# Small matmuls of a fused attention and feed-forward kernel, gathered into fewer visits of the matmul engine

## The chip, the core and the metric

The kernel runs on one core of one Trainium2 chip. The metric is device time in microseconds (us) of one execution, and the median of three runs of the kernel before is 529.8 us (529.61 to 529.82). The core has a matmul engine (TensorE, PE in the profile, with its weight loads shown apart as PEld), three elementwise engines (VectorE or DVE, ScalarE or ACT, GpSimd or POOL), a queue engine (SP) that issues all transfers here, and 16 DMA engines. TensorE writes only into PSUM, which holds eight banks of 128 x 512 words. Each engine executes its own instructions in program order and waits for others by semaphores.

## The reference

The computation is an attention against 32 pooled memories per head, followed by a bilinear feed-forward network on the attention's output:

```python
a = softmax(phi, axis=sequence)                # per batch and head: 576 x 32
k_m, v_m = a.T @ k, a.T @ v                    # 32 memories of 64
scores = q @ k_m.T / sqrt(64)                  # 576 x 32
attn = softmax(scores)                         # over the 32 memories
x = (attn @ v_m), heads side by side           # 4608 x 512 in all
out = ((x @ w1) * (x @ w2)) @ w3 @ w_out       # w1, w2: 512 x 1024
```

There are 8 batches, 8 heads, 576 rows per batch, and everything is float32 (the kernel keeps float32 accuracy by splitting numbers into a high and a low part and multiplying three times).

## The kernel before

The kernel never forms x. It uses that x @ w1 equals attn @ (v_m @ w1), so for each batch it computes a matrix **M**, the memories' values times w1 and w2, and multiplies the probabilities by M. It also computes the product W = w3 @ w_out once, at the start. M is made in four **quarters** of its columns (M0 to M3 in the tables of steps), each from a quarter of w1 and w2.

For each batch there are two long stages of full-size matmuls. The **ab stage** (`ab_stage`, line 675 for the matmuls) multiplies probabilities by M, with a scheme of seven products in place of eight, over eight column blocks f = 0 to 7. It uses for the first block the first quarter M0, and for the last two the quarter M3. Its first products are called q1 and q5, and q5 needs a bank named `o`. The **out stage** (`out_stage`, line 779) multiplies its result g by W in blocks of 128 rows. One block is 24 matmuls of 128x128 by 128x512 into one bank `o` of two, which ScalarE then copies to `osb` (line 789) and SP sends out. One `O` in the tables is a quarter of a block, six matmuls. Odd batches have five blocks, even ones four.

Between these `O`s the out stage of batch b places the attention steps of batch b+1, in the order of the table `REST`. Each name in it goes one step on with a generator:

- `blocks` turns the memories, so that lines 297 and 298 can write km (keys) and vm (values). `mem` (lines 267 and 276), which makes the memories, stands at the end of the ab stage.
- `sc0` and `sc1` (line 310) are the scores of the two halves of the rows, each 8 small matmuls of 64x32 by 64x288 (16 instructions in the trace, since a float32 matmul is issued as two). sc0 goes into the two banks of the pair `x`, sc1 into two banks `a`.
- `se`, `sn` and `pr` are the softmax on VectorE, with one exponential each on ScalarE; `pr1` ends it with a transpose into `at` (line 349).
- `ps` makes sums of the probabilities on GpSimd (line 364), their high parts on ScalarE and low parts on GpSimd (lines 366 and 367). q5 needs the last of these.
- `M0` to `M3` (`memory_weights`) have four steps: 8 small matmuls of 64x32 by 64x512 (line 386) into one bank `a` and one bank `b`; three copies on ScalarE (lines 432 and 434); six differences on VectorE (lines 437 and 439); and a cast on ScalarE (line 441) with two differences on GpSimd (line 444).
- `W0` to `W3` (`stage`, line 415) fetch a quarter of w1 and w2 back from memory, 1 MB each, into tiles that other steps use too: W0 and W3 into `kv0`, W1 into `kv2`, W2 into `q`. So W2 follows the scores, which read q, and W3 follows M0.
- `phi2`, `rows2`, `q2` and `kv2` are the loads for batch b+2.

The order on all engines is written by hand. It is the order in which the Python code runs, so the table fixes it for PE, VectorE, ScalarE, GpSimd and SP alike. The table `START` does the same for everything before the first out stage, the ab stage of batch 0 (line 646) included; its names are units A and B of that stage, steps with the batch behind a dot (`mem.1`), and others.

The PSUM banks are two `a`, two `b` (`ps_ab`), two `o` (`ps_o`) and the pair `x` (`ps_x`).

Of the kernel before, what the change touches and what calls it, by code (L numbers as in the profile page):

```python
# [36 lines left out]
K11 N1 pr0.0 W17 K12 N1 A0 K13 K10 B0 K12 A0 sc1.0 K13 A0 A4 S0 S1 L24 C23 A0 phi1 B4 A4 L25 rows1 S2 A0 A1 A4 sc1.0 A4 B1 A1  # L37
A4 N2 A1 se1.0 A1 A5 N2 A1 se1.0 B5 A5 N2 C24 se1.0 A5 A9 K10 A5 B9 sn1.0 A9 C24 sn1.0 A8 sn1.0 B8 C25 A9 pr1.0 O0 A9
A5 A8 A9 pr1.0 A8 O0 C25 pr1.0 top.1 row.1 A8 kv1 A11 kv1 B11 kv1 A8 A11 exp.1 C25 q1 A6 phi2 A11 exp.1 C25 B6 A11 A6
A3 A11 A6 B3 A3 norm.1 A6 C24 A10 A6 A3 B10 A10 C24 S3 A3 A7 A3 N3 A7 A10 A10 B7 N3 A10 O0 A7 N3 A7 A2 A7 A15 less.1 A2  # L40
B15 A15 A14 less.1 A15 A15 B14 A15 B2 A13 less.1 A2 A14 A2 A14 A13 A2 A14 less.1 B13 A14 A12 A13 A13 less.1 B12 A13
A12 mem.1 A12 A12 A12 mem.1
""".split()
MEETS = {0: "<M3 top", 1: "top exp", 2: "exp row", 3: "norm", 5: "less less", 6: "less less", 7: "less"}
REST = """
W0 W1 O blocks blocks O sc0 sc1 sc0 W2 se0 se0 sc1 se0 O se1 se1 se1 O M0 W3 phi2 rows2 sn0 sn0 sn0 pr0 M0 M0 O M1 M0 M1
sn1 sn1 sn1 pr1 O O ps M1 M2 q2 M2 O ps M1 O M2 O M3 kv2 M3 M2 O M3 M3
""".split()


# [1 line left out]
def memory_attention__then__bilinear_ffn_kernel(  # L52
# [24 lines left out]
    NT = 2  # L77
# [13 lines left out]
    ps_ab = ctx.enter_context(tc.tile_pool(name="ps_ab", bufs=2, space=bass.MemoryType.PSUM))  # L91
# [23 lines left out]
    def psum(pool, name):  # L115
        return pool.tile([P, 512], F32, name=name, tag=name)

    def psum_pair():
        return ps_x.tile([P, 2, 512], F32, name="x")

    def pair():
        x = psum_pair()
        return [x[:, i] for i in range(2)]

    def banks_ab():

        return [psum(ps_ab, x) for x in "ab"]
# [254 lines left out]
    def weights_times(b, q, w, ps):  # L382
        for g in range(NG):
            for t in range(NT):
                d = slice((1 - t) * D, (2 - t) * D)
                nc.tensor.matmul(
                    ps[t][g * M : (g + 1) * M], lhsT=vm[b % 2][d, g], rhs=w[d, :, g], start=True, stop=True
                )
# [27 lines left out]
        staged[q] = x.rearrange("p (w g f) -> p w g f", w=2, g=NG)  # L416

    def memory_weights(b, q):
        ps = banks_ab()
        weights_times(b, q, staged[q], ps)  # L420
        (b12, b11), (b21, b22) = [[x[:, k * FQ : (k + 1) * FQ] for k in range(2)] for x in ps]
        yield
        if "x" not in staged:
            staged["x"] = const.tile([P, 2, 4, FQ], F32, name="x", tag=f"w12_{NQ - 1}")
        if q == 2:
            x = const.tile([P, CW], F32, name="u", bufs=2).rearrange("p (k f) -> p k f", k=4)
        else:
            x = staged["x"][:, int(q == 1)]
        t1, t2, t3, t4 = [x[:, k] for k in range(4)]
        mh, ml = ready["M", b][q] = [new.tile([P, 7, FQ], F32R, name=f"{z}{q}") for z in ("mh", "ml")]  # L430
        firsts = ((0, 1, b11), (1, 3, ps[1].rearrange("p (k f) -> p k f", k=2)))
        nc.scalar.copy(out=t4, in_=b12)
        for i, j, y in firsts:
            nc.scalar.copy(out=mh[:, i:j], in_=y)
        yield
        for y, p, r in ((t1, t4, b11), (t3, b22, t4), (t2, b22, t1), (t4, b21, t2)):
            nc.vector.tensor_tensor(out=y, in0=p, in1=r, op=ALU.subtract)  # L437
        for i, j, y in firsts:
            nc.vector.tensor_tensor(out=ml[:, i:j], in0=y, in1=mh[:, i:j].bitcast(F32), op=ALU.subtract)
        yield  # L440
        nc.scalar.copy(out=mh[:, 3:], in_=x)  # L441
        for k in range(0, 4, 2):
            y = slice(3 + k, 5 + k)
            nc.gpsimd.tensor_tensor(out=ml[:, y], in0=x[:, k : k + 2], in1=mh[:, y].bitcast(F32), op=ALU.subtract)  # L444
# [138 lines left out]
    under_way = {}  # L583
# [161 lines left out]
    def ab_stage(b, go, before, part):  # L745
# [4 lines left out]
        for p in range(NF + 2):  # L750
            for x in order:
                if x == "+":
                    for what in MEETS.get(p, "").split():
                        if what[0] == "<":
# [48 lines left out]
    new = ctx.enter_context(tc.tile_pool(name="new", bufs=1, side="right", reuse_waits="tile"))  # L803

    def goer(b):
        begun = {}

        def go(what):
            if b + 1 == B:
                return  # L810
            if what not in begun:
                if what[0] == "M":
                    begun[what] = memory_weights(b + 1, int(what[1]))
                else:
                    begun[what] = steps[b + 1][what]()
            next(begun[what], None)

        return go
# [12 lines left out]
    def out_stage(b, go):  # L831
        ready["M", b + 1] = {}
        part, left = out_parts(b), 4 * ((S + b % 2 * REST_ROWS) // P)
        if b == 0:
            left -= 3
        next(part)
        for what in REST + left * ["O"]:
            if what == "O":
                if left > (b + 1 < B):
                    left -= 1  # L840
                    next(part)
            elif what[:-1] in LOADS:
                whole(load(what, b))
            elif what[0] == "W":
                if b + 1 < B:
                    stage(int(what[1]))
            else:
                go(what)
        return part
# [77 lines left out]
```

## Time and profile before

| What | Value |
|---|---|
| median of 3 runs | 529.8 us (529.61 to 529.82) |
| the profiled execution | 529.76 us, its span 528.0 us |
| granted TensorE clock | 1.00 (2.4 GHz) |
| PE busy | 516.9 us (98%) |
| PEld busy | 407.2 us (77%) |
| DVE busy | 360.9 us (68%) |
| ACT busy | 295.4 us (56%) |
| POOL busy | 205.4 us (39%) |
| DMA moved | 103.29 MB, 196 GB/s |

The page also shows the chain of work that ended last, the groups of instructions with their durations, and, beyond it, the trace gives a timeline, waits, and busy times of any stretch. Matmuls are pipelined, so the time one of them takes on TensorE is read from start to start in the timeline, and not from its duration. A busy PE can be a PE that drains.

### The profile page before, as it was taken

What the parts mean: (1) busy time and instruction counts of PE and PEld (TensorE: products, weight loads), DVE (VectorE), ACT (ScalarE), POOL (GpSimd) and SP (SyncE); (2) the same over time, 40 slices, a digit from 0 to 9 for tenths busy, and PEclk for the clock granted to TensorE, in tenths of its full rate; (3) what the DMA queues carried; (4) which work ended last, traced back from release to release, by engine and by line L of the source; (5) the groups of instructions that cost most, each with busy time, mean ns of one, the idle gap of its engine ahead of it and who ended that gap; (6) DMA issues with size and microseconds to landing.
All of it is one profiled execution on the core that took longest, in us unless ns stands there. A gap on an engine that the chain in (4) does not pass through costs nothing.

```text
span 528.0 us, 10212 instructions
## 1 busy us (share of the span) xinstructions
PE 516.9 (98%) x3879; PEld 407.2 (77%) x3879; DVE 360.9 (68%) x741; ACT 295.4 (56%) x574; POOL 205.4 (39%) x161
## 2 busy tenths in 40 slices
PE   8999999998999999999999999999999999999997
PEld 5447688856986699659975899669966898679986
DVE  4889999597759647695769366885768285955500
ACT  6998976437643656256625465366536364365411
POOL 0000000018641934257534924286427644195500
DMA  8999776896237810685057600783069403510011
GB/s 334 420 415 422 315 256 235 329 367 210 106 122 279 336 47 8 242 308 210 11 224 292 242 32 10 308 338 114 2 253 338 183 17 131 210 41 22 1 40 60
DMA packets 21825, 103.29 MB, mean 196 GB/s; under 512 B 2577, under 2 KB 3729, under 8 KB 12817
## 3 DMA queue, kind: packets, MB, share of 16 engines
q1 hardware_dynamic: 21776, 102.65, 50.9%
q8 instruction: 30, 0.49, 0.4%
q14 instruction: 19, 0.15, 0.1%
HBM read 89.00 MB, written 13.64 MB: 194 GB/s over the span
## 4 chain that ended last, share of the span: by engine, by line
PE 65%; DVE 22%; DMA 5%; issue 4%; ACT 2%; POOL 1%; SPq 0%; ACTq 0%; DVEq 0%
PE o L779 22%; PE b L675 13%; PE o L675 8%; PE a L675 8%; DMA kv<-in_weights 4%; DVE s_sb L341 3%; PE x L267 3%; DVE s_sb L320 2%; DVE small L327 2%; DVE s_sb L329 2%; PE a L561 2%; DVE x L437 2%; PE b L561 2%; DVE small L336 2%; DVE small L338 1%
## 5 line engine op out<-in xcount | busy, mean ns | idle before, releaser
L743 POOL TENSOR_TENSOR gl<-u,gh 128x576 fp32r<-128x576 f32 x56 | 79.7, 1428 | 105.9 <-ACT gh L740 100.8
L779 PE MATMUL o<-W,gh 128*128 128x512 f32 (+1 forms) x296 | 100.3, 393 | 0.0
L444 POOL TENSOR_TENSOR ml<-x,mh 128x512 fp32r<-128x512 f32 x42 | 53.5, 1295 | 120.2 <-ACT mh L441 120.2
L779 PEld LDWEIGHTS o<-W,gh 128*128 128x128 f32 x296 | 55.1, 188 | 25.1 <-issue 14.7
L675 PE MATMUL b<-ahl,mh 128*128 128x288 f32 x336 | 73.5, 301 | 0.2 <-DVE gr L725 0.2
L779 PE MATMUL o<-Wh,gh 128*128 128x512 f32 (+1 forms) x148 | 59.2, 400 | 0.0
L779 PE MATMUL o<-Wl,gh 128*128 128x512 f32 (+1 forms) x148 | 57.1, 386 | 0.0
L779 PE MATMUL o<-W,gl 128*128 128x512 f32 (+1 forms) x148 | 56.9, 384 | 0.0
L779 PE MATMUL o<-Wh,gl 128*128 128x512 f32 (+1 forms) x148 | 56.9, 384 | 0.0
L675 PEld LDWEIGHTS b<-ahl,mh 128*128 128x128 f32 x336 | 53.9, 188 | 2.9 <-issue 1.2
L717 DVE TENSOR_TENSOR o<-b,a_sb 128x288 f32<-128x288 f32 x56 | 25.8, 461 | 40.7 <-PE b L675 40.7
L675 PE MATMUL b<-ahl,ml 128*128 128x288 f32 x168 | 49.6, 295 | 0.0
L675 PE MATMUL o<-ahl,mh 128*128 128x288 f32 x224 | 48.3, 296 | 0.9 <-POOL ahl L367 0.9
L675 PE MATMUL a<-ahl,mh 128*128 128x288 f32 x224 | 47.8, 295 | 0.0
L694 ACT COPY b<-a 128x288 f32<-128x288 f32 x56 | 21.5, 383 | 38.4 <-DVE u L733 21.1
L789 ACT COPY osb<-o 128x512 f32<-128x512 f32 (+1 forms) x37 | 21.3, 574 | 38.6 <-PE o L779 30.6
L733 DVE TENSOR_TENSOR u<-b,gr 128x288 f32<-128x288 f32 x56 | 25.6, 458 | 24.6 <-PE b L675 24.4
L725 DVE TENSOR_TENSOR gr<-b,a_sb 128x288 f32<-128x288 f32 x56 | 25.4, 454 | 22.8 <-PE b L675 22.1
L779 PEld LDWEIGHTS o<-Wh,gh 128*128 128x128 f32 x148 | 27.8, 188 | 16.7 <-issue 11.4
L740 ACT CAST gh<-u 128x576 fp32r<-128x576 f32 x56 | 37.4, 679 | 1.6 <-DVE u L733 1.6
L675 PEld LDWEIGHTS o<-ahl,mh 128*128 128x128 f32 x224 | 36.0, 188 | 1.1 <-POOL ahl L367 1.1
L675 PEld LDWEIGHTS a<-ahl,mh 128*128 128x128 f32 x224 | 36.4, 188 | 0.6
(169 smaller groups left out, 1171.3 us busy)
## 6 DMA issues: line engine op xcount, KB each, us to landing
kv<-kept SPq DMA_DIRECT2D x21, 1024.0 KB
kv<-in_kv SPq DMA_DIRECT2D x16, 1024.0 KB, 8.2
raw<-in_weights SPq DMA_DIRECT2D x10, 1024.0 KB, 19.5
q<-in_qT SPq DMA_DIRECT2D x8, 1152.0 KB
out<-osb SPq DMA_DIRECT2D x31, 256.0 KB, 2.0
q<-kept SPq DMA_DIRECT2D x7, 1024.0 KB, 5.5
raw<-in_weights SPq DMA_DIRECT2D x12, 512.0 KB, 4.2
ph<-in_phiT SPq DMA_DIRECT2D x9, 576.0 KB, 10.0
```

Of the source, the lines that this page charges most:

```text
L267: nc.tensor.matmul(ps[t][h * M : (h + 1) * M, : 2 * D], lhsT=v["a"][:, i, t, h * M : (h + 1) * M], rhs=kvt[i][:, (4 * t + h) * 2 * D : (4 ...
L444: nc.gpsimd.tensor_tensor(out=ml[:, y], in0=x[:, k : k + 2], in1=mh[:, y].bitcast(F32), op=ALU.subtract)
L561: nc.tensor.matmul(pw[r][i], lhsT=x[:, i * P : (i + 1) * P], rhs=y, start=k == 0 and j == 0, stop=k == NF - 1 and j == len(pairs) - 1,)
L675: nc.tensor.matmul(ps, lhsT=x[:, j], rhs=y[:, i], start=start and k == 0, stop=stop and k == 2, skip_group_check=True,)
L694: nc.scalar.copy(out=self.u, in_=self.a)
L717: nc.vector.tensor_tensor(out=self.c, in0=self.u, in1=self.s5, op=ALU.add)
L725: nc.vector.tensor_tensor(out=self.c22, in0=self.u, in1=self.s5, op=ALU.add)
L733: nc.vector.tensor_tensor(out=self.gr[:, 1], in0=self.u, in1=self.c22, op=ALU.mult)
L740: nc.scalar.copy(out=self.cut(gh), in_=self.gr)
L743: nc.gpsimd.tensor_tensor(out=self.cut(gl), in0=self.gr, in1=self.cut(gh).bitcast(F32), op=ALU.subtract)
L779: nc.tensor.matmul(ps, lhsT=x[f][:, at : at + P], rhs=y[f][:, cols], start=f == 0 and k == 0, stop=f == NF - 1 and k == 2,)
L789: nc.scalar.copy(out=osb[:, cols], in_=ps)
```

## The change

Three things move; no instruction is removed or added in the stages named above, apart from where merged rows are counted.

First, `REST` takes M0's matmuls directly behind sc1's, and puts M1's, M3's and M2's directly behind one another, after six further `O`s (36 matmuls). Second, the banks: M0 now takes both banks `b`, M1 both banks `a`, M2 both banks `b`, and M3 the pair `x`, in place of one `a` and one `b` each. W3 is fetched directly behind W2. M0's differences now stand inside `sn0`, and its cast behind `ps`' first cast. Third, for batch 1 alone, `less`, `mem` and `blocks` move into the ab stage of batch 0 in `START`, between its units, and a table `REST0` of its own orders the first out stage: there the scores stand at its head, M0 stands alone 12 matmuls later, and M1, M3 and M2 follow together 30 matmuls behind it.

```diff
-A3 A11 A6 B3 A3 norm.1 A6 C24 A10 A6 A3 B10 A10 C24 S3 A3 A7 A3 N3 A7 A10 A10 B7 N3 A10 O0 A7 N3 A7 A2 A7 A15 less.1 A2
-B15 A15 A14 less.1 A15 A15 B14 A15 B2 A13 less.1 A2 A14 A2 A14 A13 A2 A14 less.1 B13 A14 A12 A13 A13 less.1 B12 A13
-A12 mem.1 A12 A12 A12 mem.1
+A3 A11 A6 B3 A3 norm.1 A6 C24 A10 A6 A3 B10 A10 C24 S3 A3 A7 A3 N3 A7 A10 A10 B7 N3 A10 O0 A7 less.1 N3 A7 A2 A7 A15 less.1 less.1 A2
+B15 A15 A14 less.1 A15 A15 B14 A15 less.1 B2 A13 A2 A14 mem.1 A2 A14 A13 mem.1 A2 A14 B13 A14 blocks.1 A12 A13 A13 blocks.1
+B12 A13 A12 A12 A12 A12
...
+REST0 = """
+W0 W1 sc0 sc1 sc0 W2 se0 se0 O sc1 se0 O se1 se1 se1 M0 W3 sn0 sn0 sn0 pr0 O M0 sn1 sn1 sn1 pr1 ps M0 phi2 rows2 O M0 O O O M1 M3 M2 q2 kv2 M1
+ps M1 M1 O M2 O M2 M2 O M3 O M3
+""".split()
 REST = """
-W0 W1 O blocks blocks O sc0 sc1 sc0 W2 se0 se0 sc1 se0 O se1 se1 se1 O M0 W3 phi2 rows2 sn0 sn0 sn0 pr0 M0 M0 O M1 M0 M1
-sn1 sn1 sn1 pr1 O O ps M1 M2 q2 M2 O ps M1 O M2 O M3 kv2 M3 M2 O M3 M3
+W0 W1 O blocks blocks O sc0 sc1 M0 sc0 W2 W3 se0 se0 se0 sc1 O M0 se1 se1 se1 sn0 sn0 M0 sn0 pr0 O sn1 sn1 sn1 pr1 ps M0 phi2 rows2 O O O O M1 M3 M2 q2 kv2 M1
+ps M1 M1 O M2 O M2 M2 O M3 O M3
 """.split()
...
     def memory_weights(b, q):
-        ps = banks_ab()
+        ps = pair() if q == 3 else [psum(ps_ab, "bab"[q]) for _ in range(NT)]
...
     def goer(b):
-        begun = {}
+        begun = {x[:-2]: step for x, step in under_way.items() if b == 0 and x.endswith(".1")}
...
-        for what in REST + left * ["O"]:
+        for what in (REST if b else REST0) + left * ["O"]:
```

The first place is TensorE in the out stage of batch 2, which prepares batch 3. Names are out<-weights or moving tile; `kv_2454` and the like are the staged quarters, and `x8` counts matmuls of the program with the same names. Before, behind the second scores:

```order
L310 MATMUL a<-q,km_83 32x288 x8
L779 MATMUL o<-W_587,gh_618 128x512
...
L386 MATMUL a<-kv_2454,vm_85 32x512
L386 MATMUL b<-kv_2454,vm_85 32x512
...
L779 MATMUL o<-Wh_90,gh_614 128x512
...
L386 MATMUL a<-kv_2456,vm_85 32x512
...
L386 MATMUL a<-q,vm_85 32x512
...
L386 MATMUL a<-kv_2535,vm_85 32x512
...
```

Now, behind the same scores (all line numbers are four higher):

```order
L314 MATMUL a<-q,km_83 32x288 x8
L390 MATMUL b<-kv_2452,vm_85 32x512 x8
L783 MATMUL o<-W_587,gh_618 128x512
...
L783 MATMUL o<-W_590,gh_621 128x512
L390 MATMUL a<-kv_2454,vm_85 32x512 x8
L390 MATMUL x<-kv_2510,vm_85 32x512 x8
L390 MATMUL b<-q,vm_85 32x512 x8
L783 MATMUL o<-Wh_90,gh_614 128x512
```

Before, the scores and the four quarters were five visits, with 12, 6, 12 and 18 matmuls of the out stage between them. Now they are two visits with 36 between them, and 42 follow the second one up to q1 (66 in the longer out stages of odd batches).

The second place is ScalarE in the same out stage, from the first cast of the probabilities on. Before:

```order
L366 CAST ahl<-at 128x864
L432 COPY u<-a 128x256
L434 CAST mh_2628<-a 128x256
...
L789 COPY osb<-o 128x512
L366 CAST ahl<-sums 128x1152
L441 CAST mh_2578<-x 128x1024
L432 COPY x<-a 128x256
...
L441 CAST mh_2628<-u 128x1024
L441 CAST mh_2682<-x 128x1024
L789 COPY osb<-o 128x512
L694 COPY b<-a 128x288
```

Now:

```order
L370 CAST ahl<-at 128x864
L445 CAST mh_2523<-x 128x1024
L793 COPY osb<-o 128x512
L436 COPY x<-a 128x256
...
L370 CAST ahl<-sums 128x1152
L445 CAST mh_2638<-x 128x1024
L436 COPY u<-b 128x256
...
L445 CAST mh_2662<-u 128x1024
L436 COPY x<-x 128x256
...
L793 COPY osb<-o 128x512
L698 COPY b<-a 128x288
```

The copies of three quarters (the second `x<-a`, `u<-b` and `x<-x`) and two of the out stage's own copies (`osb<-o`) now all stand behind the cast that waits for the softmax's end, where before two quarters had been copied ahead of it.

## Rows read from the trace of the kernel before

**Rows 1.** The page's first part: busy us, share of span, instructions of each engine.

```profile
PE 516.9 (98%) x3879; PEld 407.2 (77%) x3879; DVE 360.9 (68%) x741; ACT 295.4 (56%) x574; POOL 205.4 (39%) x161
```

**Rows 2.** The page's chain of work that ended last, by line.

```profile
PE o L779 22%; PE b L675 13%; PE o L675 8%; PE a L675 8%; DMA kv<-in_weights 4%; DVE s_sb L341 3%; PE x L267 3%; DVE s_sb L320 2%; DVE small L327 2%; DVE s_sb L329 2%; PE a L561 2%; DVE x L437 2%; PE b L561 2%; DVE small L336 2%; DVE small L338 1%
```

**Rows 3.** Waits of PE: waited for, us in total, times, longest us.

```profile
PE a L386 <- ACT mh L434: 3.5, 7, 0.5
PE o L675 <- POOL ahl L367: 0.9, 1, 0.9
```

**Rows 4.** Timeline of PE, one out stage: start us, duration us, instruction, [idle before].

```profile
217.41 0.72 PE L310 MATMUL x<-q,km 64*32 64x288 f32 x16
217.92 0.69 PE L310 MATMUL a<-q,km 64*32 64x288 f32 x16
...
221.49 0.61 PE L386 MATMUL a<-kv,vm 64*32 64x512 f32 x1
...
221.94 0.59 PE L386 MATMUL a<-kv,vm 64*32 64x512 f32 x1
...
222.51 0.50 PE L779 MATMUL o<-Wh,gh 128*128 128x512 f32 x1
...
234.19 1.01 PE L386 MATMUL a<-kv,vm 64*32 64x512 f32 x2 [0.52 <-ACT mh L434]
```

**Rows 5.** Windows: stretch, its us, busy PE, PEld, DVE, ACT, POOL, clock, DMA, GB/s.

```profile
217.41:235.86 18.45, 17.93 (x146) 10.24 (x145) 17.11 (x34) 7.53 (x16) 6.50 (x8) 1.00 0.83 315
218.54:221.49 2.95, 2.95 (x20) 2.17 (x13) 2.85 (x7) 0.69 (x1) 0.00 (x0) 1.00 0.97 342
235.86:242.79 6.93, 6.93 (x36) 5.74 (x31) 4.40 (x10) 5.47 (x8) 6.93 (x4) 1.00 0.86 336
109.30:123.67 14.37, 13.87 (x101) 7.57 (x101) 13.96 (x28) 6.42 (x14) 5.90 (x7) 1.00 0.85 318
213.50:217.50 4.00, 4.00 (x42) 2.95 (x49) 1.52 (x5) 1.76 (x4) 2.25 (x2) 1.00 0.84 287
```

**Rows 6.** Timeline of PE at the next ab stage's head: q5's first matmuls.

```profile
243.19 0.42 PE L675 MATMUL o<-ahl,mh 128*128 128x288 f32 x2
```

**Rows 7.** Timeline of DVE in that out stage: the softmax's second half.

```profile
223.69 0.18 DVE L338 TENSOR_SCALAR small<-small 128x18 f32<-128x18 f32 x1
...
224.21 0.76 DVE L341 TENSOR_TENSOR s_sb<-s_sb,small 128x576 f32<-128x576 f32 x1
...
228.83 0.85 DVE L338 TENSOR_SCALAR small<-small 128x18 f32<-128x18 f32 x1
...
230.01 1.50 DVE L341 TENSOR_TENSOR s_sb<-s_sb,small 128x576 f32<-128x576 f32 x1
231.55 0.78 DVE L349 STREAM_TRANSPOSE at<-s_sb 128x576 f32<-128x576 f32 x1
```

**Rows 8.** Timeline of POOL in that out stage.

```profile
228.37 2.53 POOL L444 TENSOR_TENSOR ml<-x,mh 128x512 fp32r<-128x512 f32 x2 [10.30 <-ACT mh L441]
232.47 0.81 POOL L364 TENSOR_TENSOR sums<-at 128x288 f32<-128x288 f32 x1 [1.57 <-DVE at L349]
...
237.65 2.70 POOL L367 TENSOR_TENSOR ahl<-sums,ahl 128x1152 fp32r<-128x1152 f32 x1
```

**Rows 9.** Timeline of ACT in that out stage.

```profile
232.36 0.92 ACT L366 CAST ahl<-at 128x864 fp32r<-128x864 f32 x1 [3.04 <-DVE at L349]
...
237.72 0.36 ACT L432 COPY x<-a 128x256 f32<-128x256 f32 x1
...
240.19 1.05 ACT L441 CAST mh<-x 128x1024 fp32r<-128x1024 f32 x1 [0.40 <-DVE x L437]
241.15 0.58 ACT L789 COPY osb<-o 128x512 f32<-128x512 f32 x1
```

**Rows 10.** Timeline of SP: the fetches of the first two quarters.

```profile
213.13 1.11 SPq L415 DMA_DIRECT2D kv<-kept  x2
```

**Rows 11.** Timeline of PEld: the weight loads of the second scores.

```profile
217.68 0.40 PEld L310 LDWEIGHTS a<-q,km 64*32 64x32 f32 x16
```

## The prediction, made before the changed kernel ran

> **What bounds the kernel now.** I read the page's first part, the chain, PE's waits, and then the timeline of one out stage. PE is busy for 98% of the span [rows 1], and the longest shares of the chain are full-size matmuls in their order on PE [rows 2]. So time comes from PE alone: from what its matmuls cost from start to start, and from its few waits. Two of these waits touch the change: 3.5 us in seven waits of a quarter of M for ScalarE, about 0.5 each, and 0.9 us, once, for the low part of the sums at q5 [rows 3].
>
> PE's busy share hides something that the timeline shows: a visit of small matmuls costs more than its streaming. The two scores follow each other after 0.51 us, and the two passes of M0 after 0.45 us, but from the second pass to the next full-size matmul it is 0.57, that is 0.12 on the way out [rows 4]. The big matmuls beside a visit lose time too. Let g be their pitch and e the loss at one border. Twelve with a border on both sides take 2.95 us (12g + 2e), thirty with one border 6.93 (30g + e) [rows 5]. That gives g = 0.227 and e = 0.11. The granted clock is 1.00 in each of these windows, so none of it is throttling. A visit thus costs 0.34 us beyond its streaming (0.12 + 2 x 0.11), though PE reads as busy.
>
> **The change, part by part.** The profiled execution took 529.76 us, against a median of 529.8, so I subtract from 529.76. I count from the start of the first scores (217.41 in before) as 0, in the out stage that prepares batch 3.
>
> *The visits.* Before, the stretch from the scores to behind M3 takes 18.45 us and holds 48 big matmuls [rows 5]. Now the same work is:
> - visit 1, scores and M0: 0.51 + 0.51 + 2 x 0.45 + 0.12 = 2.04;
> - 36 big matmuls with two borders: 36 x 0.227 + 0.22 = 8.40;
> - visit 2, three quarters: 6 x 0.45 + 0.12 = 2.82;
> - the 12 big matmuls left of the 48: 2.73.
>
> That is 15.99, so 2.46 us less. Some 1.0 of it is three visits' overhead; the other 1.4 is waiting of M2 and M3 for their banks, of which the profile names only the 0.52 before M3 [rows 4], since the rest lies inside matmuls counted as busy. The banks asked for are free in time: `x` and both `a` by the scores' transposes, and both `b` of M0 some microseconds before M2.
>
> *Batch 1.* Here M0 stands alone. The 14.37 us from M0 to behind M3 [rows 5] held 36 big matmuls. Now: M0 1.02 (221.49 to 222.51 of another batch [rows 4]), 30 big ones 30 x 0.227 + 0.22 = 7.04, visit 2 2.82, six more 1.36, together 12.24, or 2.13 less. The 0.90 before q5 [rows 3] goes as well, since both halves of the softmax now run ahead of M0's differences and the sums come sooner. `mem` and `blocks` keep their visits and get other neighbours. No row shows `blocks` six short matmuls behind `mem`; I take 0, and keep up to 1 us of loss. Sum for batch 1: 3.0.
>
> So the gross gain is 6 x 2.46 + 3.0 = 17.8 us.
>
> *What is late next.* The three quarters now reach ScalarE and GpSimd in one burst, behind the end of the softmax. Before, `pr1` ends at 231.55 + 0.78, which is 14.92. Two VectorE steps of its second half took 0.85 and 1.50 us while GpSimd worked on M0 (228.37 to 230.90); the same steps of the first half took 0.18 and 0.76 [rows 6, 7]. M0's GpSimd work now comes behind `ps`' first cast, so I take 1.41 off: `pr1` ends at 13.5.
>
> - GpSimd: from the sums' start to the end of their low part was 7.9 us (232.47 to 240.35). M0's 2.53 now goes between [rows 7]. 13.6 + 7.9 + 2.5 = 24.0.
> - ScalarE, in order: cast 0.92, M0's cast 1.05, a copy to `osb` 0.58, which is 16.0 with some overlap. A quarter takes 2.47 from its first copy to its cast (237.72 to 240.19), VectorE's differences within, and 1.05 for the cast [rows 8]: M1 to 19.5, M2 to 23.0. M3's copies take about 1.1, my estimate as less than half of these 2.47. Only then comes the `osb` copy that frees a bank `o`: 24.7 by durations, and 24.4 since neighbours overlap by some 0.1.
>
> PE reaches q5 at 2.04 + 8.40 + 2.82 + 42 x 0.227 + 0.11 + 0.40 = 23.3; the 0.40 is q1, 242.79 to 243.19 [rows 5, 9]. q5 needs that bank `o` and the sums. It waits until 24.4: 1.1 us, in three short out stages (batches 2, 4, 6). In the three long ones the fourth block needs the same bank at 2.04 + 8.40 + 2.82 + 48 x 0.227 + 0.11 = 24.3: I take 0.2 us. Everything behind q5 on PE waits with it, whole ab stage included. Bounds: no wait at all, if ScalarE's work overlaps more; and 1.41 more each, if `pr1` gains nothing. I take the values worked out from the rows. New waits: 3 x 1.1 + 3 x 0.2 = 3.9.
>
> *M0 straight behind the scores* needs its quarter from memory 1.02 us after the scores start, at 218.4 in before's time, not 221.5. Its fetch and M1's, 2.1 MB, are issued from 213.13 on [rows 10]. From 213.5 to 217.5 the transfers moved 287 GB/s, or 1.15 MB [rows 5]. If the first is served first, it has landed; if the two share evenly, the other 0.95 MB takes until 219.8, and PE waits 1.4. I take 0, as the first issued. W3, fetched directly behind W2, gets six microseconds more than it needs at this rate.
>
> Sum: 529.76 - 17.8 + 3.9 = 515.9 us.
>
> *A rule against the visits.* All groups of a visit use both 64-row halves of the array. The 16 weight loads of the second scores begin at 217.68 while the first scores still stream (to 217.92 at least), and take 0.40 [rows 11, 4]. So they are pulled ahead. The Trainium skill (TensorE: Matmul & The Clock Gate, The mechanism) says that a weight load overlaps matmuls in flight only where its row group differs. By that rule, gathered groups could not hide their loads. The trace here does not bear it out.
>
> **The rivals.**
> - *No new wait* (ScalarE and GpSimd keep up): 529.76 - 17.8 = 512.0. For it, the six overlaps that I can only guess; against it, q5 and the low sums were within a microsecond already in before (240.35 and 243.19).
> - *Weight loads that can't hide at the joints.* 20 joints (three in six batches, two in batch 1) by up to 0.40 [rows 11]: 8.0 us back, 523.9. Against it, the loads seen pulled ahead. This is what the rule just cited would give.
> - *M0's quarter is late*: 1.4 in each of six batches, 8.4 back: 524.3.
> - *The burst is later than I say.* `pr1` gains nothing: 1.41 in six batches, 8.5 back, 524.4. For it: the whole chain behind `pr1` runs on single engines in order. The Trainium skill (TensorEngine Tiling (Array Packing), PSUM Bottleneck) warns that packed matmuls speed up TensorE but not the emptying of PSUM, which may then bound. PE's waits for ScalarE agree with it [rows 3].
> - *Slower than before.* The same burst with a delay x on top of my figures eats the gain where 3 x (1.1 + x) + 3 x (0.2 + x) = 17.8, so from x = 2.3 us on, `pr1` near 15.8. It would take a softmax that M0's six differences, now inside `sn0`, hold up by more than they did before. At x = 3 the time is 533.9. Against it: VectorE has the same work ahead of `pr1` as before, and less interference.
>
> That the order is not what the change says can be left aside; the order of the instructions shows it.
>
> **How the numbers follow.** My forecast, 515.9 with its own range of 513.5 to 518.5: 0.53. No new wait: 0.17. Exposed weight loads: 0.05. Late quarter: 0.06. Late burst: 0.10. Large delay: 0.09, of which 0.02 near no change. A measurement of this kernel can tell about 0.2%, or 1 us. So faster 0.91, same 0.02, slower 0.07. From 511.5 to 522.5 the range holds the first two cases and the milder half of the next three, some 0.8. Its low end is the sum without any new wait, its high end new waits of 10 us in place of 3.9.
>
> **What would show it.** Right: the scores' visit leads into M0 with a pitch near 0.5; M1, M3 and M2 follow with 0.45 per pass and no idle time; the waits of line 386 for ScalarE are gone; the seven stretches are 2.1 to 2.5 us shorter; and in short out stages q5 waits for about 1 us, for the `osb` copy or GpSimd's low sums. Wrong: a wait before M0 for a DMA; joints of 0.8 us or more; a wait at q5 of 2 us or more, or in the long out stages too; a wait between `mem` and the scores in batch 1.

## The result, and the profile after

The changed kernel takes 515.3 us, the median of four runs (514.2 to 516.0), beside 529.7 us for the kernel before in the same session. The ratio is 0.9727, with an interval of 0.9709 to 0.9744. A later session gave 515.0 us and 0.9722 (0.9708 to 0.9735). The prediction was 515.9, in a range of 511.5 to 522.5.

A note on the row numbers in the prediction: some are off. Where it says [rows 6, 7] for the softmax and GpSimd it means groups 7 and 8, [rows 7] for M0's 2.53 us is group 8, [rows 8] for ScalarE's quarter is group 9, and [rows 5, 9] for q5 is groups 5 and 6. Groups 1 to 5, 10 and 11 are named as they stand. Below, the numbers are those of the groups as they stand. Lines from the change on are four higher than before, so L386 is now L390, and L675 is L679.

The profiled execution took 516.0 us, with a span of 514.2. The page's first part and its chain by line, to be held against [rows 1, 2]:

```profile
PE 505.9 (98%) x3879; PEld 410.7 (80%) x3879; DVE 351.5 (68%) x741; ACT 293.4 (57%) x574; POOL 205.6 (40%) x161
```

```profile
PE o L783 36%; PE b L679 13%; PE o L679 9%; PE a L679 8%; PE a L565 4%; PE b L565 4%; PE x L271 3%; DMA kv<-kept 3%; PE b L390 2%; PE o L565 2%; PE x L390 2%; DMA kv<-in_weights 2%; PE x L629 1%; PE a L390 1%; PE b L650 1%; PE x L314 1%
```

The same 3879 matmuls keep PE busy 11.0 us less (516.9 to 505.9). So most of the gain is time that had read as busy. VectorE's softmax lines, at 1 to 3% each in the chain before, are no longer among its longest.

PE's waits, in us in total, times and longest, to be held against [rows 3]:

```profile
PE o L679 <- ACT osb L793: 1.8, 3, 0.6
...
PE b L390 <- DMA kv<-kept: 0.4, 1, 0.4
PE x L390 <- DMA kv<-kept: 0.3, 1, 0.3
```

The seven waits for a bank, 3.5 us, and the one for the low sums, 0.9, have gone. Three waits for the `osb` copy are new, one in each short out stage, at q5. Twice a quarter of M waited for its fetch.

PE in the out stage of [rows 4], from the first scores on (start, duration, instruction, idle time before it):

```profile
212.71 0.71 PE L314 MATMUL x<-q,km 64*32 64x288 f32 x16
213.22 0.69 PE L314 MATMUL a<-q,km 64*32 64x288 f32 x16
213.71 1.06 PE L390 MATMUL b<-kv,vm 64*32 64x512 f32 x16
214.70 0.50 PE L783 MATMUL o<-W,gh 128*128 128x512 f32 x1
...
223.13 1.09 PE L390 MATMUL a<-kv,vm 64*32 64x512 f32 x16
224.01 1.06 PE L390 MATMUL x<-kv,vm 64*32 64x512 f32 x16
224.87 1.06 PE L390 MATMUL b<-q,vm 64*32 64x512 f32 x16
225.86 0.50 PE L783 MATMUL o<-Wh,gh 128*128 128x512 f32 x1
...
235.52 0.42 PE L679 MATMUL a<-ahl,mh 128*128 128x288 f32 x2
...
236.69 0.53 PE L679 MATMUL o<-ahl,mh 128*128 128x288 f32 x2 [0.61 <-ACT osb L793]
```

The scores run straight into M0 (0.51, 0.48), and M1, M3 and M2 follow each other at 0.88 and 0.86, two passes each. There is no idle time inside a visit and none at its joints. The last of these rows is q5 with its wait. The 0.61 is what the view calls idle; from q1's start to the next `O` the time went from 0.79 to 1.67, so the wait costs 0.88.

The windows of that stage (us, then busy PE, PEld, DVE, ACT, POOL, clock, DMA share, GB/s), for [rows 5]:

```profile
212.71:225.86 13.15, 13.15 (x133) 8.27 (x132) 11.91 (x24) 2.87 (x6) 0.66 (x1) 1.00 0.90 346
214.70:223.13 8.43, 8.43 (x45) 6.68 (x37) 8.19 (x17) 2.87 (x6) 0.00 (x0) 1.00 0.95 350
225.86:235.52 9.66, 9.66 (x50) 7.99 (x43) 5.21 (x13) 8.07 (x14) 9.28 (x8) 1.00 0.65 234
```

From the first scores to q1 it is 13.15 + 9.66 = 22.81, where it was 18.45 + 6.93 = 25.38. The clock is 1.00 as before. In the last window GpSimd is busy for 9.28 of 9.66 us and ScalarE for 8.07. That is the burst of the three quarters.

VectorE, GpSimd and ScalarE there, for [rows 7 to 9]:

```profile
223.94 0.17 DVE L342 TENSOR_SCALAR small<-small 128x18 f32<-128x18 f32 x1
...
224.45 0.76 DVE L345 TENSOR_TENSOR s_sb<-s_sb,small 128x576 f32<-128x576 f32 x1
225.24 0.78 DVE L353 STREAM_TRANSPOSE at<-s_sb 128x576 f32<-128x576 f32 x1
...
237.71 1.01 DVE L443 TENSOR_TENSOR ml<-x,mh 128x256 fp32r<-128x256 f32 x2
...
239.30 0.45 DVE L721 TENSOR_TENSOR o<-b,a_sb 128x288 f32<-128x288 f32 x1
```

```profile
231.38 2.55 POOL L448 TENSOR_TENSOR ml<-x,mh 128x512 fp32r<-128x512 f32 x2
233.89 2.67 POOL L371 TENSOR_TENSOR ahl<-sums,ahl 128x1152 fp32r<-128x1152 f32 x1
```

```profile
226.05 0.91 ACT L370 CAST ahl<-at 128x864 fp32r<-128x864 f32 x1 [6.56 <-DVE at L353]
...
234.07 1.06 ACT L445 CAST mh<-u 128x1024 fp32r<-128x1024 f32 x1 [1.28 <-DVE u L441]
235.02 0.37 ACT L436 COPY x<-x 128x256 f32<-128x256 f32 x1
235.28 0.86 ACT L438 CAST mh<-x 128x256 fp32r<-128x256 f32 x2
236.03 0.61 ACT L793 COPY osb<-o 128x512 f32<-128x512 f32 x1
```

The softmax's two steps take 0.17 and 0.76 again, no longer 0.85 and 1.50, since GpSimd works on M0 only later. Counted from the first scores, `pr1` ends at 225.24 + 0.78 - 212.71 = 13.31, the low sums at 23.85 and `osb` at 23.93. ScalarE idles 1.28 of those while VectorE makes M2's differences.

The first scores of batches 1 to 7 start at 105.22, 157.20, 217.41, 272.17, 332.48, 387.26 and 447.45 us in the trace of before, and at 102.82, 154.90, 212.71, 265.91, 324.31, 377.49 and 435.25 in the trace after. The differences of the intervals show where the time came from:

| Stretch | Gain, us | Predicted |
|---|---|---|
| start to batch 2's scores (batch 1's preparation) | 2.30 | 3.0 |
| the three with a long out stage | 2.40, 1.91, 2.43 | 2.26 each |
| the three with a short one | 1.56, 1.60, 1.60 | 1.36 each |
| sum | 13.8 | 13.9 |

The first row holds chance, too. Up to some 97 us both kernels run the same matmuls in the same order; the last of them starts at 97.11 us in the trace before and at 97.25 in the trace after. Counted from there to batch 2's scores, batch 1 gained 2.44 (60.09 to 57.65).

### The profile page after: what moved, and what is told of

Its sections match the earlier page's. It is cut to its first block, busy times and chain, and to the rows that moved or that the text cites. A ratio compares the mean times of both kernels' runs of the same rounds, so it can differ in the third digit from the quotient of the medians.

```text
span 514.2 us, 10164 instructions
## 1 busy us (share of the span) xinstructions
PE 505.9 (98%) x3879; PEld 410.7 (80%) x3879; DVE 351.5 (68%) x741; ACT 293.4 (57%) x574; POOL 205.6 (40%) x161
## 4 chain that ended last, share of the span: by engine, by line
PE 91%; DMA 4%; DVE 2%; ACT 1%; issue 1%; SPq 0%; POOL 0%; POOLq 0%; ACTq 0%; DVEq 0%
PE o L783 36%; PE b L679 13%; PE o L679 9%; PE a L679 8%; PE a L565 4%; PE b L565 4%; PE x L271 3%; DMA kv<-kept 3%; PE b L390 2%; PE o L565 2%; PE x L390 2%; DMA kv<-in_weights 2%; PE x L629 1%; PE a L390 1%; PE b L650 1%; PE x L314 1%
## 5 line engine op out<-in xcount | busy, mean ns | idle before, releaser
L783 PE MATMUL o<-W,gh 128*128 128x512 f32 (+1 forms) x296 | 97.6, 387 | 0.0
L679 PE MATMUL b<-ahl,mh 128*128 128x288 f32 x336 | 74.0, 302 | 0.2 <-DVE gr L729 0.2
L368 POOL TENSOR_TENSOR sums<-at 128x288 f32<-128x288 f32 x14 | 11.3, 807 | 134.4 <-DVE at L353 134.4
L679 PEld LDWEIGHTS b<-ahl,mh 128*128 128x128 f32 x336 | 53.8, 188 | 3.3 <-issue 1.2
L679 PE MATMUL o<-ahl,mh 128*128 128x288 f32 x224 | 48.3, 297 | 1.8 <-ACT osb L793 1.8
L679 PE MATMUL b<-ahl,ml 128*128 128x288 f32 x168 | 49.6, 295 | 0.0
L679 PE MATMUL a<-ahl,mh 128*128 128x288 f32 x224 | 47.8, 295 | 0.0
L679 PEld LDWEIGHTS o<-ahl,mh 128*128 128x128 f32 x224 | 35.9, 188 | 2.5 <-ACT osb L793 2.5
L679 PEld LDWEIGHTS a<-ahl,mh 128*128 128x128 f32 x224 | 36.4, 188 | 0.6
```

The lines of the kernel that those rows point to most:

```text
L679: nc.tensor.matmul(ps, lhsT=x[:, j], rhs=y[:, i], start=start and k == 0, stop=stop and k == 2, skip_group_check=True,)
L783: nc.tensor.matmul(ps, lhsT=x[f][:, at : at + P], rhs=y[f][:, cols], start=f == 0 and k == 0, stop=f == NF - 1 and k == 2,)
```

## The experiments

The theory: the gain has two sources, visits of about 0.34 us each and waits for banks, and what is given back is the burst behind the softmax, in which ScalarE's `osb` copy and GpSimd's low sums both come just after PE wants q5. The rivals: it is the banks alone; the joints or neighbours cost something of their own; batch 1's own table matters little; or what is given back can't be had by another order. All ratios are against the kernel before.

**Banks alone.** The kernel before with the new assignment of banks; the five visits stay.

```
     def memory_weights(b, q):
-        ps = banks_ab()
+        ps = pair() if q == 3 else [psum(ps_ab, "bab"[q]) for _ in range(NT)]
```

> The kernel before with one edit: M0 takes both banks b, M1 both banks a, M2 both banks b, M3 the pair x, while the order and the five visits stay. My theory says that of the 2.46 us per out stage about 1.4 are waits of M2 and M3 for their banks and 1.0 is three visits' overhead. Then six out stages get 1.4 us shorter each, and batch 1 gains nothing, since q5 there still waits for the low sums: 529.7 - 8.6 = 521.1 us, with no idle time of PE ahead of line 386 and 12.6 to 13.0 us from M0 to behind M3 where before had 14.4. The rival, that gathering into visits is all that counts and the banks matter only because a gathered visit needs them, expects 529.7. A second rival, that the bank waits were nearly all, expects 515 to 517.

Measured: 523.9 us (523.0 to 524.5), ratio 0.9889 (0.9873 to 0.9905), 2.8 us above what was expected. The direction held, the size did not. PE's timeline and waits:

```profile
227.35 1.31 PE L386 MATMUL b<-q,vm 64*32 64x512 f32 x16
...
232.90 1.09 PE L386 MATMUL x<-kv,vm 64*32 64x512 f32 x16
```

```profile
PE o L675 <- POOL ahl L367: 1.6, 1, 1.6
```

M3 now takes 1.02 in place of 1.66, and the 18 matmuls before it 4.31 in place of 4.89: 1.22 us per stage. M2 still takes 1.24 where M0 takes 1.02, so 0.22 stay, since it now waits for the banks `b` that VectorE empties of M0 (until 227.42 us, while M2 starts at 227.35). And what PE gained, q5 took back in part: in batch 1 its wait grew from 0.9 to 1.6, and in the three short stages, where q5 had not waited, the time from q1 to the next `O` grew from 0.78 to 1.03, with q5 right behind the `osb` copy (which ends at 241.34; q5 starts at 241.40). So the 2.46 of a stage split into about 1.0 for three visits, 1.22 for M3 and 0.22 for M2.

**Five visits with the new banks.** The changed kernel with one `O` set between sc1 and M0, M1 and M3, M3 and M2, in batches 2 to 7.

```
-... O sc0 sc1 M0 sc0 W2 W3 se0 se0 se0 sc1 O M0 ... O O O O M1 M3 M2 q2 kv2 M1
+... O sc0 sc1 O M0 sc0 W2 W3 se0 se0 se0 sc1 M0 ... O O O O M1 O M3 O M2 q2 kv2 M1
```

> The changed kernel with its visits split again by one O each: sc1 O M0, and M1 O M3 O M2, for all batches but the first prepared; banks, fetches and all other orders as changed, and the same count of matmuls. My theory gives each of the three further visits 0.34 us beyond streaming, so the stretch from the scores to behind M2, at an equal number of big matmuls, gets 1.0 us longer in six out stages. In the three short ones the wait at q5 (0.88 us in the changed kernel) shrinks by as much, since ScalarE's copies don't move. So 3 x 1.0 + 3 x 0.15 = 3.5 us more than the changed kernel: about 518.8. If borders cost nothing, it stays at 515.3; if the drain is a microsecond per visit, it is 521 to 524.

Measured: 518.9 us (518.8 to 519.3), ratio 0.9798 (0.9782 to 0.9815), as expected. From the first scores to behind M2 one window, now with 48 matmuls of the out stage:

```profile
213.23:230.22 16.99, 16.99 (x146) 9.91 (x145) 12.73 (x26) 6.62 (x13) 4.11 (x6) 1.00 0.72 277
```

The changed kernel's 13.15 holds 36 of them. With 12 more at 0.227 it would be 15.87, so three visits cost 1.12, or 0.37 each, against 0.34 by the borders of before. PE reads as busy in all of it. No wait at q5 is left in this kernel: PE simply comes 1.1 us later. So per short stage only 0.2 of the three visits' gain remains, and the rest had gone into q5's wait.

**The general table for batch 1 too.** The changed kernel with `START` of before and `REST` for all batches.

```
-A3 ... O0 A7 less.1 N3 A7 A2 A7 A15 less.1 less.1 A2
+A3 ... O0 A7 N3 A7 A2 A7 A15 less.1 A2
...
-        for what in (REST if b else REST0) + left * ["O"]:
+        for what in REST + left * ["O"]:
```

> The changed kernel without its part for batch 1: START as before (mem and blocks at its end), and REST in place of REST0 in the first out stage. Batches 2 to 7 are as changed. In the first out stage 24 big matmuls are left between the second visit and q1. By the chain of the prediction PE reaches q5 19.2 us after the scores begin, while the low sums end at 23.9 there: a wait of 4.7 us. That makes batch 1 about 1.2 us longer than in the kernel before, where the changed kernel gained 2.3: 515.3 + 3.5 = 518.8 us (517.5 to 520). If the burst behind the softmax isn't what q5 waits for, the wait is under 2 us and the time at most 516.

Measured: 520.5 us (519.4 to 521.1), ratio 0.9824 (0.9808 to 0.9841), half a microsecond beyond the expected range. PE in batch 1's out stage:

```profile
120.73 0.50 PE L783 MATMUL o<-Wh,gh 128*128 128x512 f32 x1 [0.86 <-ACT osb L793]
...
128.84 0.41 PE L679 MATMUL o<-ahl,mh 128*128 128x288 f32 x1 [3.19 <-POOL ahl L371]
```

In this shorter first out stage (24 matmuls behind the second visit, where the others have 42) the same burst makes PE wait 4.05 us (0.86 and 3.19). Counted from the last matmul that all these kernels have at the same place, batch 1 takes 61.46 us up to batch 2's scores, against 60.09 before and 57.65 in the changed kernel. So the gathered visits alone would have made batch 1 slower by 1.4 us, and its own order is worth 3.8, more than the 2.4 by which batch 1 gained.

The next three try to get q5's 0.88 us back by moving single steps; the changed kernel was measured once more beside them.

> The changed kernel once more, as the base for the three beside it: 515.3 us (514.2 to 516.0 so far), with q5 waiting about 0.9 us in the three short out stages and never in the long ones. Its runs differed by 1.8 us where the kernel before differs by 0.3; the one profile so far shows waits of the small matmuls for a fetched quarter, 0.3 in batch 1 and 0.4 in one other batch. If these make the difference, another profile has them at other places or sizes.

Measured: 515.0 us (514.5 to 515.7), ratio 0.9722. Its profile has the three waits at q5 (1.9 us in all) and lists no wait of M for a fetch, though M0 of batch 4 is late here too: it starts 1.26 us after the first scores, where the other batches have 1.00. Its span is 512.7, 1.5 less than in the first profile. The late fetches are the smaller part of this: the last matmul ahead of everything that the change moves starts at 96.14 here and at 97.25 there, 1.1 us apart, and from it to the end the two take 416.6 and 416.9. Over the fourteen profiles of this document that matmul starts between 96.1 and 97.7. So most of the difference between executions arises in the first 97 us, where the change moves no matmul.

**`osb` ahead of M3's copies.** Edit in `REST`:

```
-ps M1 M1 O M2 O M2 M2 O M3 O M3
+ps M1 M1 O M2 O M2 M2 O O M3 M3
```

> The changed kernel with one step moved: in REST, M3's copies on ScalarE come one O later, so the copy to osb that frees q5's bank stands ahead of them. By the trace q5's bank is then free at least 0.7 us sooner, but its second matmul still needs the low sums on GpSimd, which end at 236.56 where q5 could begin at 235.92: the wait moves from ScalarE to GpSimd and shrinks from 0.88 to about 0.6 us. 3 x 0.3 = 0.8 us less than the changed kernel: 514.5. If the copy were the only cause, 2.6 us less: 512.7.

Measured: 515.6 us (514.8 to 517.2), ratio 0.9735 (0.9717 to 0.9753).

```profile
PE o L679 <- POOL ahl L371: 1.2, 3, 0.4
```

The wait went over to GpSimd's low sums, as expected, but only 0.19 of 0.88 us was saved. And the ab stage behind it grew by 0.3 (21.47 to 21.82), with a new wait of 0.16 for VectorE's L721. So the gain of 0.8 us was not seen: 515.6, beside 515.0 for the changed kernel. (The profiled execution, at 517.2, also has one M0 that waits 1.3 us for its fetch.) GpSimd's is a second chain, which ends 0.1 us from the first.

**M0's last step ahead of `pr0`, in addition.**

```
-... sn0 sn0 M0 sn0 pr0 O sn1 sn1 sn1 pr1 ps M0 phi2 ...
+... sn0 sn0 M0 sn0 M0 pr0 O sn1 sn1 sn1 pr1 ps phi2 ...
```

> The same, and M0's cast on ScalarE and its low parts on GpSimd come ahead of the softmax's second half (inside REST, before pr0), so that they no longer stand between the softmax's end and the low sums. GpSimd's work ahead of the low sums gets 2.5 us shorter, of which 0.7 to 1.4 goes back because VectorE's second half runs slower beside it, as in the kernel before. The low sums end 1.1 to 1.8 us sooner and the osb copy about 1 us: no wait at q5, 3 x 0.88 = 2.6 us less than the changed kernel, 512.7. If VectorE loses the full 1.41, up to 0.3 us of wait stays: 513.5. If the order of GpSimd's work doesn't matter, it equals the run before it, 514.5.

Measured: 517.2 us (516.4 to 517.3), ratio 0.9758 (0.9745 to 0.9771). The expectation was wrong by 4.5 us. q5's wait has only halved (in two of the three short stages q1 to the next `O` takes 1.18, where the changed kernel has 1.67 and 0.79 would be without a wait), and another stands right behind it:

```profile
PE b L679 <- DVE o L721: 2.4, 3, 1.0
```

```profile
224.24 0.95 DVE L342 TENSOR_SCALAR small<-small 128x18 f32<-128x18 f32 x1
...
239.06 1.01 DVE L443 TENSOR_TENSOR ml<-x,mh 128x256 fp32r<-128x256 f32 x2
...
240.65 0.45 DVE L721 TENSOR_TENSOR o<-b,a_sb 128x288 f32<-128x288 f32 x1
```

GpSimd's two differences of M0 (2.83 us from 222.33 on) again lie beside VectorE's L342, which takes 0.95 in place of 0.17, and counted from the first scores (213.01 here) `pr1` ends 0.8 us later than in the changed kernel. GpSimd's low sums end 1.7 us sooner, as expected, but `osb` only 0.5, since ScalarE waits 0.95 for GpSimd's sums. M3's copies stand behind `osb`, as in the run before, so its differences end at 27.06, where it was 26.01 in the changed kernel and 26.50 in the run before. VectorE's first step of the ab stage, L721, follows them in order and is late.

**The second visit of batch 1 later, in addition** (one more `O` ahead of `M1 M3 M2` in `REST0`).

> The same, and in REST0 alone the second visit comes one O (six matmuls, 1.4 us) later, behind the landing of M3's quarter, for which PE waited 0.8 us in all in the changed kernel's profile. 0 to 0.8 us less than the run before it, as the wait is there in some runs only: about 512.3. If q5 in batch 1 then waits for the burst behind the visit, it is up to 1 us more: 513.7.

Measured: 517.8 us (517.3 to 518.0), ratio 0.9771 (0.9758 to 0.9784). Wrong as well: the wait for L721 now stands in batch 1 too.

```profile
PE b L679 <- DVE o L721: 3.4, 4, 1.0
```

Up to here no new order had won the wait back. The next runs take the burst apart. In three of them (cast apart, low on VectorE, copies filled in) the lines up to 443 are two lower than in the changed kernel.

**M0's cast apart.** Its cast on ScalarE stands ahead of `pr0`, its differences stay where they were.

```
         nc.scalar.copy(out=mh[:, 3:], in_=x)
+        if q == 0:
+            yield
         for k in range(0, 4, 2):
...
-... sn0 sn0 M0 sn0 pr0 ...
+... sn0 sn0 M0 sn0 M0 pr0 ...
```

> The changed kernel with M0's last step cut in two: its cast on ScalarE stands ahead of pr0, where ScalarE idles, and its two GpSimd differences stay where they were, behind the first casts of ps. Nothing reaches GpSimd earlier, so VectorE's steps of the softmax keep their 0.17 and 0.76 us and pr1 does not move. Theory (ScalarE's chain behind the softmax was the last at q5 and, copied late, made VectorE late at L721): ScalarE has 1.04 us less behind the cast of the probabilities, the osb copy ends near 235.6 in the changed kernel's time in place of 236.64, M3's differences end 1 us earlier, so nothing is given back one instruction later. GpSimd's low part of the sums still ends at 236.5, so q5 in the three short stages waits for GpSimd and the wait falls only from 0.88 to about 0.8: 515.1. Rival (the delay of the run with M0's whole step ahead of pr0 came from the cast itself on ScalarE): L721 waits about 1 us in three stages: 517.5.

Measured: 514.7 us (514.5 to 515.7), ratio 0.9716 (0.9702 to 0.9730). The time is as expected, but the changed kernel's 0.9722 lies in this interval, so no gain is shown. The rival (the cast itself does the harm) fell: no wait for L721. But the way there was not as expected. ScalarE in that stage:

```profile
229.57 1.16 ACT L368 CAST ahl<-sums 128x1152 fp32r<-128x1152 f32 x1 [0.94 <-POOL sums L366]
...
235.94 0.61 ACT L793 COPY osb<-o 128x512 f32<-128x512 f32 x1
```

The 1.04 us that ScalarE was spared turned into waiting for GpSimd's sums, 0.94 us, at the next cast. Counted from the first scores (212.85 here), `osb` ends at 23.70 in place of 23.93, and q5 still waits 0.70 us for it, not for GpSimd.

**M0's differences on VectorE, in addition.**

```
-            nc.gpsimd.tensor_tensor(out=ml[:, y], ...
+            (nc.gpsimd if q else nc.vector).tensor_tensor(out=ml[:, y], ...
```

> As the run with M0's cast apart, and M0's two differences go from GpSimd to VectorE, which idles for 2.96 us behind the softmax's last transpose in the changed kernel; all seven batches. Theory (q5 waits for what is last of ScalarE's and GpSimd's chains): GpSimd's low part of the sums ends 2.55 us earlier, near 234.0, ScalarE's osb copy near 235.6; PE is at q5 at 235.9, so the wait there goes, three times 0.88, and M3's differences on VectorE end earlier too: 515.2 - 2.6 = 512.6. Rival 1 (VectorE then is late: M0's two differences take 2.5 us beside GpSimd's sums and push M1's, M2's and M3's back): the wait comes back as one of q for VectorE's L721, 515 to 516. Rival 2 (the wait is a matter of total work, not of order): no change, 515.2.

Measured: 518.6 us (517.9 to 520.6), ratio 0.9792 (0.9771 to 0.9814). Wrong by 6 us. GpSimd, ScalarE and PE's waits:

```profile
234.77 2.69 POOL L369 TENSOR_TENSOR ahl<-sums,ahl 128x1152 fp32r<-128x1152 f32 x1
```

```profile
232.83 1.16 ACT L368 CAST ahl<-sums 128x1152 fp32r<-128x1152 f32 x1 [1.57 <-POOL sums L366]
```

```profile
PE o L679 <- ACT osb L793: 3.0, 3, 1.0
PE b L679 <- DVE o L721: 1.4, 1, 1.4
```

GpSimd's low sums did come earlier: counted from the first scores (215.49 here) they end at 21.97, while PE is at q5 at 23.2. But its first two sums took 1.10 and 1.15 us beside VectorE's differences, in place of 0.81 (the last section shows them), so ScalarE's cast of the sums waited 1.57 us, 0.63 more than in the run before. `osb` came 0.6 us later than there, and 0.4 later than in the changed kernel. In batch 1 a wait of 1.4 for L721 came on top, and 1.0 us of waits for fetches in this profile. Rival 1 named VectorE as what would be late; in batches 2 to 7 it was ScalarE, waiting for GpSimd.

**M1's fetch later.** The changed kernel with W1 placed behind M0's matmuls in the table.

```
-W0 W1 O blocks blocks O sc0 sc1 M0 sc0 W2 ...
+W0 O blocks blocks O sc0 sc1 M0 W1 sc0 W2 ...
```

> The changed kernel with the fetch W1 issued behind M0's matmuls in place of right behind W0, in batches 2 to 7. Theory (the two fetches share the DMA engines, and in some executions M0's quarter lands after PE reaches it, which makes up part of the 1.8 us between fast and slow executions of the changed kernel): M0's quarter lands about 2 us earlier, no wait of M0 for a DMA in the profile, and the median is 514.6 to 515.0 with a smaller spread. Rival (the spread comes from elsewhere): 515.2 with the same spread. Loss if M1's quarter is now late: M1 stands about 9 us behind M0 and a fetch takes 5.5, so none expected.

Measured: 515.9 us (514.9 to 516.3), ratio 0.9730 (0.9715 to 0.9745). The edit did not do what was meant. SP still issues the two fetches right behind each other, without waiting for PE's M0: in batch 4 at 261.70 and 262.14 us here, and at 261.63 and 262.07 in the changed kernel, while M0 starts only at 267.35. So for SP this is the changed kernel a third time, with the same spread and a wait of 0.2 for the same fetch (M0 of batch 4 starts 1.37 us after the first scores). Whether M1's fetch beside it makes M0's quarter late was not tested, and the cause stays open.

**The two chains together.** M0's differences on VectorE (batch 1 excepted), and ScalarE's `osb` copy and M3's copies moved ahead of M2's cast. Against the changed kernel, beside the edits of M0's cast apart:

```
-ps M1 M1 O M2 O M2 M2 O M3 O M3
+ps M1 M1 O M2 O O O M3 M2 M2 M3
...
+            (nc.vector if b > 1 and q == 0 else nc.gpsimd).tensor_tensor(out=ml[:, y], ...
```

> Two changes on top of the changed kernel, each against one of the two chains that end last at q5. As in the run with M0's differences on VectorE (in batch 1 they stay on GpSimd here), and the table's tail becomes ps M1 M1 O M2 O O O M3 M2 M2 M3: on ScalarE the osb copy and M3's copies stand ahead of M2's cast, in the 1.28 us in which ScalarE waited for VectorE's differences of M2. Theory (in-order waiting on ScalarE for GpSimd's sums, 1.57 us, and for VectorE's M2, 1.28 us, is what makes osb late): counted in the changed kernel's time, osb ends near 233.7, GpSimd's low sums near 234.7, VectorE's last difference of M3 near 237.9 instead of 238.7, and PE is at q5 at 235.9: no wait there and none at L721 behind it, 515.2 - 3 x 0.88 = 512.6. Rival (what is removed here comes back on VectorE, which carries 1.87 us more): a wait for L721 of about 1 us in three stages, 515 to 518.

Measured: 512.6 us (511.9 to 513.0), ratio 0.9680 (0.9666 to 0.9693), as expected, and the best of all. ScalarE, VectorE and PE in that stage:

```profile
232.10 0.61 ACT L793 COPY osb<-o 128x512 f32<-128x512 f32 x1
...
233.58 1.11 ACT L443 CAST mh<-u 128x1024 fp32r<-128x1024 f32 x1
```

```profile
235.76 1.01 DVE L441 TENSOR_TENSOR ml<-x,mh 128x256 fp32r<-128x256 f32 x2
...
237.36 0.47 DVE L721 TENSOR_TENSOR o<-b,a_sb 128x288 f32<-128x288 f32 x1
```

```profile
234.94 0.43 PE L679 MATMUL o<-ahl,mh 128*128 128x288 f32 x2
```

Counted from the first scores (211.74 here), `osb` ends at 20.97 where it was 23.93, and PE starts q5 at 23.20 without idle time. ScalarE's cast of M2 no longer waits, for M3's copies fill the 1.28 us, and VectorE is done with M3 at 25.03 where it was 26.01. No wait at q5 or L721 remains in any short stage.

**The tail alone**, without moving anything to VectorE.

> The changed kernel with only the table's tail changed, ps M1 M1 O M2 O O O M3 M2 M2 M3: ScalarE's osb copy and M3's copies ahead of M2's cast. M0's differences stay on GpSimd, between the two low parts of the sums. Theory (two chains end within 0.1 us of each other at q5): osb ends about 1.5 us earlier, q5 then waits for GpSimd's low sums, 0.7 us in each of three stages, and M3's copies and differences stand 0.7 us earlier or more, so nothing is given back at L721: 515.2 - 3 x 0.2 = 514.6. Rival (ScalarE's copy alone was the limit): no wait at q5, 512.6.

Measured: 515.0 us (514.4 to 516.3), ratio 0.9728 (0.9714 to 0.9741), 0.4 above what was expected.

```profile
PE o L679 <- POOL ahl L371: 1.3, 3, 0.4
```

The wait at q5 went from ScalarE to GpSimd and stayed at 0.69. So neither chain's edit alone wins the 2.6 us, and both together do: there were two chains, and only the run that shortens both has the gain. One combination was not run, the tail together with M0's cast apart and nothing on VectorE. The trace here speaks against it: counted from the first scores (212.27), GpSimd works from 13.45 to the end of the low sums at 23.87 with no gap above 0.1 us, so an edit on ScalarE can't bring them forward.

## Why the prediction was right, and where not

- *What bounds the kernel* held. The gain came out of PE's own time. Over the whole execution it is 11.0 us of what had read as busy and 2.8 of idle time, but that mixes in the first 97 us. From the last common matmul on (97.11 and 97.25) PE's busy time fell by 12.2 us (423.1 to 410.9) and its idle time by 1.7: the 4.4 us of waits that went, less the new ones.
- *Visits*: 0.34 was worked out from the borders, and the run with five visits shows 0.37. The three predicted lengths 2.04, 8.40 and 2.82 became 1.99 (212.71 to 214.70), 8.43 and 2.73. From scores to q1 a stage gained 2.57, where 2.46 was predicted. About 0.1 us of it is lost again in the ab stage behind it (21.47 against 21.37), which was not followed further.
- *Banks*: 1.4 per stage held. 1.22 of it came with the banks alone; M2's 0.22 went only when the visits moved too (M2 takes 0.99 in the changed kernel). So "free in time" is true for M2 only because of them.
- *Joints*: no loss. The Trainium skill (TensorE: Matmul & The Clock Gate, The mechanism) would hide a weight load only behind matmuls of another row group. The rows do not show it here: 0.88 and 0.86 for two passes, none of them with idle time. That rival, 523.9, is out.
- *The burst* came as predicted, at the place and by the engines named: `pr1` at 13.31 (13.5), low sums at 23.85 (24.0), `osb` at 23.93 (24.4). The rivals "burst later" and "slower" are out, since VectorE's steps took 0.17 and 0.76. The warning of the Trainium skill (TensorEngine Tiling (Array Packing), PSUM Bottleneck), that emptying PSUM may bound packed matmuls, agrees in a small way: ScalarE, which empties the quarters' banks and the banks `o`, is late with `osb` three times. "No new wait" is half true: nothing in the long stages (0.2 predicted), 0.88 in the short ones (1.1). What was held against that rival was misread: in the kernel before, the low sums ended at 240.35 and q5 started at 243.19, 2.8 us apart and not "within a microsecond". The waits came even so, for the reasons in the sum.
- *Mis-sized: batch 1.* Predicted 3.0, measured 2.3, or 2.4 without the first 97 us, and 2.6 in the second profile counted in the same way. The 0.90 at q5 did go. But in both profiles the scores waited 0.2 for the matmul ahead of them, and the 12 matmuls between scores and M0 took 3.21 in place of 2.95. In the first one M3 also waited for its fetch (0.29 idle, the visit 0.53 longer).
- *Mis-sized: the fetch of M0's quarter*, taken as 0. In one batch of the profiled execution it was late:

```profile
267.50 1.09 PE L390 MATMUL b<-kv,vm 64*32 64x512 f32 x15 [0.39 <-DMA kv<-kept]
```

  That is 0.6 us from start to start (1.08 in place of 0.48). In the second profile it is 0.26, in the same batch, number 4. So that rival happens in one batch, and not in all six; its cause is open. Its price of 1.4 goes by 401 to 419 GB/s, which the trace has from 215.5 to 220 us but no row shows.

The misses cancel: 0.7 too much for batch 1 (0.1 of it from the first 97 us) and 0.5 too little for a late fetch, against six stages that otherwise each gained about 0.2 more than predicted. So the sum of 13.9 against 13.8 is better than its terms, and that it is so close is luck.

## What to carry to other kernels

Look for time inside a busy engine: start-to-start pitches at the borders of a group of small matmuls showed here what gathering them is worth, before any run. When work is gathered, lay out in order what the other engines get in one burst, and find every chain that ends at the next thing PE needs; where two end within 0.1 us, shortening one shows little (here 0.2 of 0.9 us). And an engine that stands in the middle of its burst waiting for another, as ScalarE for 1.28 us, is where the next instruction that waits for nothing belongs.

## What the runs showed of the hardware

VectorE and GpSimd slow each other in both directions, and by the form of the instruction. Beside GpSimd's differences a VectorE step on 128x18 took 0.95 in place of 0.17 us. Beside VectorE's 128x512 differences of M0, GpSimd's sums took 1.10 to 1.15 in place of 0.81. VectorE's 128x256 differences, which have one operand in PSUM and run beside GpSimd all through the burst, kept their 1.01 for two, and its reciprocals on 128x18 in SBUF their 0.27.

The Trainium skill (Trainium Architecture — The Big Picture, What this means for kernel authors) says that VectorE and GpSimd share one pair of ports, as an exclusive lock. The traces agree with waiting for another's turn. In the run with M0's cast ahead of `pr0`, the small step of 0.95 ends at 225.19 us, 0.03 behind GpSimd's difference (225.16), and so it is, to 0.04, each time that it is slowed there and in the kernel before. In the run with M0's differences on VectorE the two engines take turns:

```profile
228.72 1.87 DVE L448 TENSOR_TENSOR ml<-x,mh 128x512 fp32r<-128x512 f32 x2
228.94 1.10 POOL L366 TENSOR_TENSOR sums<-at 128x288 f32<-128x288 f32 x1 [12.80 <-DVE at L351]
230.12 1.15 POOL L366 TENSOR_TENSOR sums<-sums,at 128x288 f32<-128x288 f32 x1
```

The view merges VectorE's two differences. Taken apart, they last from 228.72 to 229.37 us (0.65) and from 229.29 to 230.59 (1.30). The first sum ends 0.67 us behind the first difference, the second difference 0.55 behind that sum, and the second sum again 0.67 behind that difference. Batches 2 to 7 all show this. The lines overlap, so an instruction that waits for its turn counts as busy here.
